# Sliding-window attention and a gated layer on one core: q and k loaded two tokens a partition, a narrower last stage, biases by ScalarE, the last block in halves

## The chip, the core and the metric

The kernel runs on one core of one Trainium2 chip. The metric is device microseconds of one execution, lower is better. The core has TensorE (PE; its weight loads are shown apart as PEld), VectorE (DVE), ScalarE (ACT), GpSimd (POOL) and SyncE (SP), each with an instruction queue worked off in order, and 16 DMA engines that move data between the device's memory (HBM) and the on-chip memory (SBUF). TensorE writes its results into PSUM, eight banks of 512 float32 columns on 128 partitions.

## What is computed

Attention over 8 batches, 8 heads, 576 tokens, head size 64, each token seeing itself and the 127 before it, with a bias that falls with the distance at a slope of its own for each head; then a gated layer over the 4608 tokens with all heads side by side (512 columns).

```python
scores = scale * np.matmul(q, k.transpose(0, 1, 3, 2))
bias = slopes[:, None, None] * (-np.abs(rel).astype(np.float32))[None, :, :]
mask = (rel >= 0) & (rel < window)            # window = 128
scores = np.where(mask, scores + bias[None], -1000000000.0)
...
attn = np.exp(scores)
attn = attn / (np.sum(attn, axis=-1, keepdims=True) + 1e-09)
x = np.matmul(attn, v)                        # then (B*S, H*D)
H = np.maximum(x @ w_h, 0.0)
T = 1.0 / (1.0 + np.exp(-(x @ w_t + b_t)))
out = T * H + (1.0 - T) * x
```

## The kernel before

**The order.** Nothing is scheduled by a planner at build time: `ORDER` (line 18) is a string of three-character steps, a letter and a two-digit number, and the loop at the end (line 433) issues them one after the other. Each engine works off its own steps in that order; semaphores hold a step until what it reads is there and what it overwrites has been read. `BANKS` (line 44) names the first PSUM bank of every tile in the order in which they are taken (`take`, line 247). The steps:

- `L`, `V`, `W`: loads of q or k, of v, of the weights (`load`, line 145), issued from POOL's queue, cast from float32 to bf16 on the way. `B` (line 224) loads the bias as float32 on all partitions from SP's queue.
- `T`: the transpose of a q or k tile on DVE (`tr`, line 233).
- `s`, `e`, `m`: scores on PE, exp on ACT, multiply by mask and bias table on DVE, one per stage (`scores`, `soft`, `mask`, lines 254 to 300). There are 32 stages, four per batch; each takes four PSUM banks, one for two heads: three stages of 2 x 192 columns a bank and a last one of 2 x 256.
- `p`, then `y` or `Y`: the two halves of P times V on PE for a block (`pv`, line 310; `Y` puts a drain of PE, a fence, ahead of the second half). There are 36 blocks of 128 tokens: four per batch, and one more per pair of batches made of both batches' last 64 tokens.
- `n`: division by the row sum on DVE. `x`, `c`: the block's transposes on PE and their copy by ACT. `h`: x times w_h on PE. `z`: x times w_t on PE, with the bias added by a fifth matmul against a matrix of ones (line 393), or, if `b` came before, onto the bias that ACT copied into the bank (`bias`, line 378; in 12 blocks).
- `u` or `U`: ReLU minus x, by DVE in one instruction (`u`, line 368), or ReLU by ACT (`U`, line 372) and the subtraction by DVE (`v`, line 374). `a`: tanh on ACT. `t` or `D`: half the tanh plus a half, by ACT or by DVE. `g` or `G`: the product, by DVE or POOL. `O` or `o`: plus x, by DVE or POOL. `d`: the store from SP's queue.
- `J`, `R`, `P`, `Q`, `S`, `r`, `I`, `k`, `K`: set-up, that is zeroing, the distances, the identity (`I`, on POOL), the tables (`k`, on ACT) and 22 matmuls on zeros that keep PE busy (`K`).

**q and k.** A load of one of them fills a tile of 4 heads by 32 partitions; a partition holds 18 neighbouring tokens (4608 bytes of HBM in one piece, 2304 bytes in SBUF). There are two tiles per batch and tensor, 32 loads and 32 transposes in all. The transpose takes 32x32 blocks of 4-byte pairs and writes token s*18+t of a block at place s*18+t, so neighbours of one block land 18 pairs, 72 bytes, apart. Tiles `LD` and `TR` (lines 110 and 112) are there twice, for even and odd batches: a load of batch b+2 waits for the transposes of batch b, a transpose for the scores of two batches earlier.

**v.** One load per batch into `va`, of 64-value rows; all eight batches have their own room. From the second part of the kernel on, a load of v starts behind a DVE operation named by `between` (line 137); POOL's gates and adds do so too.

**Start and end of the order:**

```
Q00L00B00R00S00L01r00L02L03J00k00P00K00L04L05L06L07T00V00T01W00L08T02I00W01T03s00W02T04s01e00L09T05e01s02V01T06 ...
... z35O33U35g34d33v35O34a35D35d34g35O35d35
```

Of the kernel before, what the change touches and what calls it, by code (L numbers as in the profile page):

```python
# [9 lines left out]
P = 128  # L10
# [4 lines left out]
ADD = ()  # L15
# [3 lines left out]
    "Q00L00B00R00S00L01r00L02L03J00k00P00K00L04L05L06L07T00V00T01W00L08T02I00W01T03s00W02T04s"  # L19
    "01e00L09T05e01s02V01T06e02s03T07e03L10m00s04m01s05e04m02L11m03p00e05p01Y00Y01n00p02L12n0"  # L20
    "1x00Y02c00p03n02x01V02h00c01m04x02y03c02h01n03U00s06m05L13x03L14e06z00T08h02c03T09a00s07"
    "t00v00z01u01e07g00m06h03U02p04m07a01p05Y04t01Y05n04z02U03G01b03n05z03L15a02T10V03x04p06a"
    "03T11p07c04Y06t02Y07n06z04o01n07s08a04D03x05v02e08x06D04x07T12h04c05s09v03c06m08h05c07T1"
    "3G03e09z05u04G02h06U05T14a05s10o00b06p08T15e10Y08o03d00z06d01n08U06L16s11m09a06x08e11m10"
    "h07v05z07u07o02c08s12a07m11L17d02p09d03e12p10Y09Y10G04n09t05s13n10L18p11e13o04T16Y11x09x"
    "10L19c09n11d04s14c10V04h08m12e14h09m13U08s15m14b08h10e15g05T17o05z08u10z09a08d05v06t06m1"
    "5p12a09p13Y12t07x11n12U09z10G07c11T18t09x12y13o07a10p14p15n13Y14b11Y15L20c12v08p16n14t10"
    "G06z11n15h11a11o06T19x13x14c13y16L21d06p17c14n16d07L22x15h12L23c15D11g10U11s16D08U12g08y"
    "17v09z12e16n17G09T20x16h13a12o08c16s17b14u13z13L24d08e17v11L25m16z14t12T21o10p18a13s18a1"
    "4m17L26Y18t13h14n18e18G13z15T22o09U14p19a15s19b16v12V05d09Y19m18e19d10z16n19h15o13T23a16"  # L30
    "x17x18c17p20L27g12U15T24Y20G11c18s20z17n20e20o11T25h16o12t15d11s21a17u16x19e21d12h17D14v"
    "14d13m19h18U17z18c19T26G14U18x20m20L28h19a18c20D16s22T27b19G16p21e22Y21u19o14z19n21s23L2"
    "9v15d14a19m21L30p22e23h20g15D17z20m22U20v17x21m23p23c21p24y22a20Y23n22o15z21n23o16d15p25"
    "a21y24Y25t18n24G17p26d16t19x22n25h21c22L31v18x23x24U21v20y26g19x25b22D20h22g18c23g20n26o"
    "17z22t21c24u22h23V06a22d17v21c25s24T28U23z23e24O19h24D22O18a23m24s25d18b24d19h25e25v23D2"
    "3z24G23u25U24T29x26z25G22c26a24T30s26o20a25z26e26T31d20h26m25a26s27U26g21m26p27e27p28Y27"
    "Y28v24n27o21t24n28s28V07d21x27e28v26p29g24x28m27Y29c27s29c28n29o22h27e29h28m28d22U27p30o"
    "23u28s30b27Y30e30o24d23x29n30z27c29v27d24s31m29a27z28e31m30h29D26D25g26a28g25p31m31p32t2"
    "8x30z29c30D27U29g28g27p33a29o25y31y32n31h30b30n32d25x31z30c31O28p34O26a30y33Y34U30D29d26"
    "n33p35t30h31v29g29x32z31v30c32n34o29b32x33u31y35c33x34o27n35z32a31g30h32d27a32D31d28g31c"  # L40
    "34d29z33O30t32O31d30U32x35h33a33d31v32c35g32z34D33U33O32v33h34d32a34g33h35t34u34z35O33U3"
    "5g34d33v35O34a35D35d34g35O35d35"
)
BANKS = (
    "1404040642740106057405613572357067450674075047506406540540567507256320742534074507640674"
    "0671450740574357045064520326105307546054067150750640754076407605730625723310567540271570"
    "1"
# [3 lines left out]
def lists():  # L51
# [8 lines left out]
    for b in range(NB):  # L60
        loads += [(w, b, g) for g in range(NG) for w in "kq"]
        loads += [("v", b)]
        if b == 0:
            loads += [("w", 0), ("w", 1), ("w", 2)]
# [8 lines left out]
def kernel(  # L73
# [55 lines left out]

    paired = [None]  # L130

    scaled = [None]

    def alone(ins):
        paired[0] = ins.ins
# [34 lines left out]
    def pads(i):  # L170
        for g in range(NG):
            for w in "qk":
                zero(TR[i, g, w][:, S:SQ, :])

# [303 lines left out]
```

## Time and profile before

| what | us |
|---|---|
| median of 3 runs | 156.6 |
| lowest and highest of them | 156.53 and 159.39 |
| the profiled execution | 156.13 |
| its span, first to last instruction | 154.2 |
| TensorE busy | 130.4 |
| VectorE busy | 136.0 |
| ScalarE busy | 121.3 |
| GpSimd busy | 80.8 |

The profile is of one execution. The 1.93 us between the execution and its span lie around the first and the last instruction. Busy times are unions of the engine's instructions; matmuls overlap each other, so the mean duration of one (380 ns for 512 columns) is longer than the pace at which they follow (four of them in 0.86 us). A group's line gives line number, engine, operation, output and input tiles and shapes, the count, then busy time and the mean of one in ns, then the idle time ahead of them and what ended it. The chain of work that ended last is followed back from the last instruction: at each step to what released it, or to the instruction before it on its engine; "issue" is time in which the engine waited for nothing that the profile shows. Tiles in PSUM are all called `ps`.

### The profile page before, as it was taken

The page shows a single profiled execution, that of the slowest core. Times are in us where ns is not written, and L with a number is a line of the kernel's source. Part 1 is how long each engine was busy: PE and PEld are TensorE (multiplying, and loading weights), DVE is VectorE, ACT ScalarE, POOL GpSimd, SP SyncE. Part 2 cuts the span into 40 slices and gives each one's busy share as a digit, 9 for nine tenths or more (in the row PEclk, how much of TensorE's full clock was granted, in tenths as well). Part 3 has the DMA queues.
Part 4 walks back from the last instruction along what each step waited for, and adds up shares of the span by engine and source line. Part 5 has one row for each costly group of instructions (what it writes and reads, how often), then busy time and mean ns, then how long its engine had stood idle before and what let it go on. Part 6 is the DMA issues. An engine that isn't in the chain of part 4 may idle for free.

```text
span 154.2 us, 6207 instructions
## 1 busy us (share of the span) xinstructions
PE 130.4 (85%) x2694; PEld 71.8 (47%) x2728; DVE 136.0 (88%) x257; ACT 121.3 (79%) x178; POOL 80.8 (52%) x90
## 2 busy tenths in 40 slices
PE   0598658698998999998999999989999799999930
PEld 0233326344554555465545545466445554555410
DVE  4999948398999899997999999989999979999880
ACT  3655972299579999994999999868999999868830
POOL 6984414402909479279488957554753771204000
PEclk9999995999999999999999999999999999999995
DMA  4999999999999759997999998786599199042732
GB/s 70 197 206 207 161 198 210 160 196 167 189 175 65 197 107 204 189 185 142 127 223 231 221 183 232 137 161 168 101 129 229 68 133 233 6 138 108 302 136 68
DMA packets 48106, 25.30 MB, mean 164 GB/s; under 512 B 38224, under 2 KB 39248, under 8 KB 48080
## 3 DMA queue, kind: packets, MB, share of 16 engines
q0 software_dynamic: 42688, 15.21, 91.6%
q1 hardware_dynamic: 5392, 9.70, 18.5%
q8 instruction: 21, 0.34, 0.9%
q14 instruction: 5, 0.04, 0.1%
HBM read 30.67 MB, written 9.44 MB: 260 GB/s over the span
## 4 chain that ended last, share of the span: by engine, by line
PE 70%; DMA 10%; issue 6%; DVE 6%; ACT 5%; DVEq 0%
PE ps L389 19%; PE ps L362 19%; PE ps L333 14%; DMA va<-in_v_dram 10%; PE ps L269 8%; PE ps L352 6%; PE ps L393 3%; ACT r L293 2%; ACT p L293 1%; DVE ot L417 1%; PE ps L279 1%; DVE p L168 1%; DVE uu L412 0%; DVE x L343 0%; ACT tt L402 0%
## 5 line engine op out<-in xcount | busy, mean ns | idle before, releaser
L417 POOL TENSOR_TENSOR ot<-uu,x 128x512 f32<-128x512 bf16 x26 | 29.8, 1155 | 23.8 <-DVE uu L376 9.6
L293 ACT ACTIVATE p<-ps 128x1536 bf16<-128x1536 f32 x24 | 34.7, 1457 | 4.6 <-PE ps L269 4.3
L362 PE MATMUL ps<-wH,xt 128*128 128x512 bf16 x130 | 35.3, 382 | 1.6 <-issue 1.0
L389 PE MATMUL ps<-wT,xt 128*128 128x512 bf16 x127 | 35.4, 380 | 1.1 <-issue 0.3
L412 POOL TENSOR_TENSOR uu<-uu,tt 128x512 bf16<-128x512 bf16 x14 | 16.1, 1153 | 23.8 <-ACT tt L402 10.6
L357 ACT COPY xt<-ps 128x512 bf16<-128x512 bf16 x36 | 20.6, 587 | 9.9 <-PE ps L352 9.7
L397 ACT ACTIVATE tt<-ps 128x512 f16<-128x512 f32 x36 | 21.6, 602 | 7.0 <-PE ps L393 4.7
L343 DVE TENSOR_TENSOR x<-ps,rd 128x512 bf16<-128x512 f32 x36 | 24.9, 691 | 2.1
L333 PE MATMUL ps<-va,p 64*128 64x65 bf16 x768 | 22.2, 193 | 3.9 <-DMA va<-in_v_dram 1.3
L300 DVE TENSOR_TENSOR p<-p,mk 128x1536 bf16<-128x1536 bf16 x24 | 22.8, 970 | 0.0
L333 PEld LDWEIGHTS <-p 64*128 64x128 bf16 x768 | 16.6, 95 | 12.6 <-issue 10.2
L362 PEld LDWEIGHTS <-xt 128*128 128x128 bf16 x144 | 13.0, 99 | 14.2 <-issue 1.8
L389 PEld LDWEIGHTS <-xt 128*128 128x128 bf16 x144 | 12.6, 98 | 12.9 <-issue 0.6
L154 POOL DMA_DIRECT2D va<-in_v_dram x8 | 14.8, 1851 | 1.9 <-DMA ld00k<-in_k_dram 1.0
L293 ACT ACTIVATE r<-ps 128x2048 bf16<-128x2048 f32 x8 | 15.0, 1874 | 0.5
L372 ACT ACTIVATE uu<-ps 128x512 bf16<-128x512 f32 x24 | 14.4, 604 | 1.0 <-PE ps L362 0.9
L352 PE MATMUL ps<-ident,x 128*128 128x128 bf16 x144 | 13.7, 225 | 1.5 <-issue 1.2
L342 DVE RECIPROCAL rd<-ps 128x8 f32<-128x8 f32 x36 | 7.1, 198 | 7.6 <-PE ps L333 7.1
L352 PEld LDWEIGHTS <-x 128*128 128x128 bf16 x144 | 9.5, 99 | 6.3 <-issue 1.9
L402 ACT ACTIVATE tt<-tt 128x512 f16<-128x512 f16 x19 | 11.9, 632 | 0.1
L242 PE MATMUL ps<-spin 128*128 128x512 bf16 x22 | 7.2, 503 | 5.4 <-DVE spin L168 5.4
L300 DVE TENSOR_TENSOR r<-r,mk 128x2048 bf16<-128x2048 bf16 x8 | 10.3, 1294 | 0.3 <-ACT r L293 0.3
(77 smaller groups left out, 195.2 us busy)
## 6 DMA issues: line engine op xcount, KB each, us to landing
out_dram<-ot SPq DMA_DIRECT2D x32, 256.0 KB, 4.0
va<-in_v_dram POOLq DMA_DIRECT2D x8, 576.0 KB, 10.9
ld00k<-in_k_dram POOLq DMA_DIRECT2D x4, 288.0 KB, 5.7
ld00q<-in_q_dram POOLq DMA_DIRECT2D x4, 288.0 KB, 6.0
ld01k<-in_k_dram POOLq DMA_DIRECT2D x4, 288.0 KB, 6.1
ld01q<-in_q_dram POOLq DMA_DIRECT2D x4, 288.0 KB, 7.1
ld10k<-in_k_dram POOLq DMA_DIRECT2D x4, 288.0 KB, 5.8
ld10q<-in_q_dram POOLq DMA_DIRECT2D x4, 288.0 KB, 7.5
```

The costliest lines, as they stand in the source:

```text
L154: ins = nc.gpsimd.dma_start(out=va[:, b, :, 0:D], in_=v[b].rearrange("h s d -> (h s) d").rearrange("(n p) d -> p n d", p=P))
L293: nc.scalar.activation(out=pview(b, s), in_=SC.pop((b, s))[:, :, 0:n].rearrange("p h (g n) -> p h g n", g=NG), func=ACTF.Exp, scale=scale)
L300: alone(nc.vector.tensor_tensor(out=p, in0=p, in1=(MK3 if s == 3 else MK)[:], op=ALU.mult))
L333: mm = nc.tensor.matmul(out=av[o : o + m, par, j * (D + 1) : (j + 1) * (D + 1)], lhsT=PT[bb, st][rows, h, c : c + m], rhs=VA[bb][rows, at ...
L343: nc.vector.tensor_tensor(out=x[:].rearrange("p (i r d) -> p r i d", i=NH, r=2), in0=av[:, :, :, 0:D], in1=rd[:].to_broadcast([P, 2, NH, D ...
L352: nc.tensor.transpose(out=pt[:, c * P : (c + 1) * P], in_=X[b, s][:, c * P : (c + 1) * P], identity=ident[:])
L357: nc.scalar.copy(out=xt[:].rearrange("p c n -> p (c n)"), in_=XP.pop((b, s)))
L362: nc.tensor.matmul(out=pa, lhsT=XT[b, s][:, c, :], rhs=wH[:, c, :], start=c == 0, stop=c == NC - 1)
L389: nc.tensor.matmul(out=pz, lhsT=xt[:, c, :], rhs=wT[:, c, :], start=c == 0 and not given, stop=c == NC - 1 and given, skip_group_check=given)
L397: nc.scalar.activation(out=tt[:], in_=PZ.pop((b, s)), func=ACTF.Tanh, scale=0.5)
L412: note(eng.tensor_tensor(out=uu, in0=uu, in1=TT.pop((b, s))[:], op=ALU.mult))
L417: note(eng.tensor_tensor(out=ot[:], in0=UU.pop((b, s))[:], in1=X[b, s][:], op=ALU.add))
```

## The change

Five edits and a new `ORDER` and `BANKS` (both strings are left out below).

- q and k: batch 0 is loaded as before, into halves of a wider tile. For batches 1 to 7 a load brings 2 heads into 32 partitions, a partition getting 18 pieces of 2 tokens (512 bytes of HBM each, 256 in SBUF); four loads fill a tile of all 8 heads, and one transpose per tensor turns it. `L` goes from 32 to 60, `T` from 32 to 18. A transpose of batches 1 to 7 has 1152 pairs a partition, and neighbours land 2 pairs, 8 bytes, apart. Heads lie in another order in the tiles, which `scores`, the tables and `pv` follow.
- The last stage of a batch: 448 columns instead of 512 (the last 64 tokens against themselves once, each of the two head groups on its own half of the partitions). Exp writes a tile of its own (`E3`), and the multiply is two instructions into `PE3`; the second table `MK3` (8 activations to set up) gives way to a small `MT`.
- `b` goes from 12 to 32 blocks; `z` of the other 4 keeps the matmul.
- The last block of all (35): after the first half of its columns come steps `f`, `w`, `q`, `j`, `l`, which do h, u, g, O and the store for columns 256 to 511. One of its two row halves is stored from ACT's queue.
- The bias load `B` waits for the latest transpose of batch 0 (`turned`); the tiles `xt` have six buffers instead of four; an option that was switched off (`ADD`, `additive`) is gone.

The new order moves work between engines. Steps of each kind:

| step | L | T | b | u | U | v | D | t | g | G | O | o | Y | y |
|---|---|---|---|---|---|---|---|---|---|---|---|---|---|---|
| before | 32 | 32 | 12 | 12 | 24 | 24 | 17 | 19 | 22 | 14 | 10 | 26 | 25 | 11 |
| after | 60 | 18 | 32 | 28 | 8 | 8 | 20 | 16 | 27 | 9 | 12 | 24 | 31 | 5 |

Its start and its end:

```
L00P00L01L02J00S00R00K00L03L04r00L05k00L08T00L09Q00L06L07L10T02T01L11T03V00s00B00s01W00e00W01e01s02W02V01T04s03e02T05L12e03L13m00s04m01s05e04m02L16m03I00p00 ...
... z35t34u34g34d33h35a35o34f00u35t35w00g35d34q00O35j00d35l00
```

```diff
     for b in range(NB):
-        loads += [(w, b, g) for g in range(NG) for w in "kq"]
+        loads += [(w, b, h) for w in "kq" for h in (0, 2, 1, 3)] if b else [
+            (w, b, g) for g in range(NG) for w in "kq"]
...
-    fx = ctx.enter_context(tc.tile_pool(name="fx", bufs=4))
+    fx = ctx.enter_context(tc.tile_pool(name="fx", bufs=6))
...
     def load(kind, *at):
         if kind in "qk":
-            b, g = at
+            b, h = at
+            if b == 0:
+                half = LD[0, kind][:].rearrange("p n x -> p (n x)")[:, h * NT * D : (h + 1) * NT * D]
+                nc.gpsimd.dma_start(
+                    out=half, in_=(q if kind == "q" else k)[0, h::NG].rearrange(
+                        "h (s t) d -> h s (t d)", t=NT))
+                return
             nc.gpsimd.dma_start(
-                out=LD[b % 2, g, kind][:],
-                in_=(q if kind == "q" else k)[b, 4 * g : 4 * g + 4].rearrange(
-                    "h (s t) d -> (h s) (t d)", t=NT))
+                out=LD[b % 2, kind][32 * h : 32 * h + 32],
+                in_=(q if kind == "q" else k)[b, NG * h : NG * h + NG].rearrange(
+                    "g (n s t) d -> s (g n) (t d)", s=32, t=2))
...
     def tr(w, b, g):
...
         nc.vector.transpose(
-            out=TR[b % 2, g, w][:, 0:S].rearrange("p s e -> p (s e)").bitcast(U32).rearrange(
-                "p (s t) -> p t s", t=NT),
-            in_=LD[b % 2, g, w][:].bitcast(U32).rearrange("p (t i) -> p t i", i=32))
+            out=TR[b % 2, w][:, 0 : NG * S].rearrange("p s e -> p (s e)").bitcast(U32).rearrange(
+                "p (n s t) -> p n t s", s=32, t=2),
+            in_=LD[b % 2, w][:].rearrange("p n x -> p (n x)").bitcast(U32).rearrange(
+                "p (n t i) -> p n t i", t=2, i=32))
...
     def mask(b, s):
-        p = pview(b, s)
-        alone(nc.vector.tensor_tensor(out=p, in0=p, in1=(MK3 if s == 3 else MK)[:], op=ALU.mult))
+        p = pview(PT[b, s])
+        if s < 3:
+            alone(nc.vector.tensor_tensor(out=p, in0=p, in1=MK[:], op=ALU.mult))
+            return
+        e3 = E3[b % 2]
+        nc.vector.tensor_tensor(out=p, in0=e3[:, :, 0:384].rearrange("p h (g n) -> p h g n", g=NG),
+                                in1=MK[:], op=ALU.mult)
+        alone(nc.vector.tensor_tensor(out=PT[b, s][:, :, 576:640], in0=e3[:, :, 384:448], in1=MT[:], op=ALU.mult))
...
+    LAST = (NB // 2 - 1, NS)
+
+    def cols(b, s, half):
+        if (b, s) != LAST:
+            return slice(0, DM)
+        return slice(half * DM // 2, (half + 1) * DM // 2)
...
+            eng = nc.scalar if r and (b, s) == LAST else nc.sync
+            eng.dma_start(out=out[row : row + D, at], in_=ot[r * D : (r + 1) * D, at])
+
+    second = dict(f=mm_h, w=lambda b, s, half: relu_sub(b, s, "u", half), l=store,
+                  q=lambda b, s, half: gate(b, s, "g", half), j=lambda b, s, half: add_x(b, s, "O", half))
```

## The prediction

> **What bounds the kernel now.** I read the page's busy times first, then the chain of work that ended last, then busy times by stretch of the span, then the groups with shapes kept apart.
>
> ```profile
> PE 130.4 (85%) x2694; PEld 71.8 (47%) x2728; DVE 136.0 (88%) x257; ACT 121.3 (79%) x178; POOL 80.8 (52%) x90
> ...
> q0 software_dynamic: 42688, 15.21, 91.6%
> ...
> PE 70%; DMA 10%; issue 6%; DVE 6%; ACT 5%; DVEq 0%
> ```
>
> By busy time VectorE leads; by the chain TensorE does. The chain from 0 to 36 us and its lines from 32 to 146 us say which holds where:
>
> ```profile
> 6.80 15.12 DMA va<-in_v_dram
> 21.93 0.14 issue
> 22.06 0.55 PE ps L333 x24
> ```
> ```profile
> by line: PE ps L389 25.8%; PE ps L362 23.7%; PE ps L333 16.6%; PE ps L269 10.4%; PE ps L352 7.0%; issue 4.7%; PE ps L393 4.3%; ACT r L293 3.2%; ACT p L293 1.3%; PE ps L279 1.3%; ACT tt L402 0.6%; ACT xt L357 0.5%; ACT tt L397 0.4%; ACT uu L
> ```
> ```profile
> 32.00:142.00 110.00, 103.75 (x2262) 58.33 (x2289) 104.55 (x184) 98.30 (x141) 63.91 (x62) 1.00 1.09 159
> ```
>
> Three stages. Until 22.06 us TensorE's P times V waits for the first v load: issued at 6.80 us, behind eight q, k loads, landed 15.12 us later. From there to about 146 us TensorE's own matmuls are 89% of the chain (25.8+23.7+16.6+10.4+7.0+4.3+1.3). The last row (length, then busy PE, PEld, DVE, ACT, POOL) shows VectorE as full as TensorE, 104.55 and 103.75 of 110 us, and ScalarE at 98.30. So PE sets the end, and DVE would as soon as it got more work. The tail runs from the last matmul near 147.8 us to 154.2. The profiled execution took 156.13 us (span 154.2 and 1.93 around it), 0.3% under the median 156.6; I sum against 156.13.
>
> **The change part by part.** Prices:
>
> ```profile
> L368 DVE SCALAR_TENSOR_TENSOR uu<-ps,x 128x512 bf16<-128x512 f32 x12 | 8.2, 683 | 0.6 <-PE ps L362 0.4
> L376 DVE TENSOR_TENSOR uu<-uu,x 128x512 bf16<-128x512 bf16 x24 | 10.3, 431 | 0.2 <-ACT uu L372 0.2
> L393 PE MATMUL ps<-bT,ones 128*128 128x512 bf16 x24 | 9.1, 379 | 0.2 <-issue 0.2
> L380 ACT COPY ps<-bA 128x512 f32<-128x512 f32 x12 | 7.2, 601 | 0.2
> L372 ACT ACTIVATE uu<-ps 128x512 bf16<-128x512 f32 x24 | 14.4, 604 | 1.0 <-PE ps L362 0.9
> L234 DVE STREAM_TRANSPOSE tr10k<-ld10k 128x576 uint32<-128x576 uint32 x4 | 5.0, 1253 | 0.0
> L168 DVE MEMSET bT<- 128x256 uint32 x1 | 0.3, 272 | 0.0
> L181 DVE MEMSET va<- 128x288 bf16 x1 | 0.3, 298 | 1.0 <-issue 1.0
> L148 POOL DMA_DIRECT2D ld10k<-in_k_dram x4 | 2.3, 571 | 1.3 <-DVE rd L342 1.3
> L160 POOL DMA_DIRECT2D wH<-in_moe_w_h_dram x1 | 0.8, 779 | 0.0
> L154 POOL DMA_DIRECT2D va<-in_v_dram x8 | 14.8, 1851 | 1.9 <-DMA ld00k<-in_k_dram 1.0
> ```
>
> Transposes. 28 of 1.245 us (34.9 us) become 14 of 1152 elements. The old row costs 2.06 ns an element after some 0.05 us; the memset of 256 uint32 costs 1.06 with everything in it. What sets the transpose apart from the engine's other rows is where it writes: neighbouring elements 72 bytes apart (18 tokens of 4 bytes). The new one writes them 8 bytes apart. Lower end: 1.06 ns, 1.22 us each. Upper end: 2.06 ns, 2.42 us. Both a contiguous write and a 4-byte element at 1.06 ns exist (L168), so I take 1.25 us: 14 x 1.25 = 17.5, DVE -17.4 us. Against it stands L181, which writes 130 bytes apart and still takes 298 ns for 288 elements: a wide step alone need not cost double. At the upper end DVE gains 1.0 us only. The Trainium skill ("SBUF — State Buffer", Specifications) says that a 16-byte line needs two hits for full bandwidth; by that, 72 bytes pay and 8 bytes do not, and the sum would be the lower end's. L181 is a row that disagrees with it, the 2.06 ns one that agrees.
>
> ReLU moved. U (ScalarE, then v on DVE) falls 24 to 8, u (DVE alone) rises 12 to 28: ACT -16 x 0.604 = -9.7, DVE 16 x (0.683 - 0.431) = +4.0.
>
> Bias by ScalarE, 12 to 32: ACT +20 x 0.601 = +12.0. PE loses 20 of 24 bias matmuls; on the chain these are 4.3% of 114 us = 4.9 us, so 20/24 of it, -4.1 us, lies on the path.
>
> Gates and adds. D 17 to 20, t 19 to 16: ACT -1.9, DVE +0.85. G 14 to 9: POOL -5.8, DVE +5 x 0.416 = +2.1. o 26 to 24: POOL -2.3, DVE +2 x 0.682 = +1.4. Halves of the last block: DVE +0.4.
>
> Last stage of a batch. Exp over 1792 columns: between the rows for 1536 (1.457 us) and 2048 (1.874), 1.67: ACT 8 x -0.2 = -1.7. The multiply is one of 1536 (0.970) and one of 256 (0.28, from 0.970 at 1536 and 0.416 at 512) against 1.294: nothing. The 16 extra score matmuls stay 16. The table set-up loses 8 activations (ACT -2.1) in front of the first exp, which waited for PE anyway: no gain.
>
> Sums. DVE after the start: -17.4+4.0+0.85+2.1+1.4+0.4 = -8.7 us; at the transpose's upper end +7.7. ACT in the steady stage: +12.0-9.7-1.9-1.7 = -1.3. PE: -4.1.
>
> POOL. 28 issues of 128 rows (0.57) become 56 of 576 pieces. Between 0.57 and v's 1.85 (4608 pieces); nearest is the weight's 0.78 (512 pieces), so 0.8: 44.8 - 16.0 = +28.8, with the gates and adds +20.7, 101.5 us in all. It is an in-order queue on which G, o and the loads wait for each other; room is there (63.91 of 110 us busy). What hangs on it is the stores, and the six `ft` buffers: if its adds come later than that, tanh and ReLU wait for a buffer.
>
> DMA. Bytes stay; packets on q0 go to 42688 - 28 x 128 + 56 x 576 = 71,360. The trace's packet records: 128-byte packets take 31 ns and start at up to 1,208 per us, 2304-byte ones 192 ns and 92 per us, that is 13.2 and 174 ns of an engine each. A line between puts 256 bytes at 23 ns by rate, 41 ns by duration. q and k of a batch: 4608 packets over 16 engines, 6.6 us (by duration 11.8) against 5.6 now. The steady stage has the room (the transfers' bytes pass well under the 233 GB/s of the best slice); the start has not: batch 1 lies ahead of the first v. +1.0 us there, up to +6; the bias broadcast (256 KB, now issued behind the first transposes) leaves the start, -0.7. Net +0.3, and +0.2 for the smaller pieces' issue: V00 +0.5 us. The queue's SP side: the bias load now waits some 12 us on SP, with no store behind it before about 41 us.
>
> Order. The identity's select on POOL now stands behind V01 and three loads; it is needed by the first block transpose near 24 us, and POOL's issues up to it sum to about 18 us from 1.3 us on (12 loads 8.7, v 3.7, weights 2.1, three loads 2.4, the iota 0.6), so it stays hidden, with some 4 us to spare; beyond that it delays PE one for one. Fenced P times V: 25 to 31; a fence shows as 0.08 us of "issue" (22.61 us in the chain): +0.5.
>
> Gaps. In the steady stage 12.4 of 114 us on the chain are not matmuls (issue 5.4, ACT 7). Bounds: nothing to half. With DVE 8% lighter, six `fx` buffers for four, and ACT no fuller, I take a fifth: -2.5.
>
> Tail. Last DVE work after the last matmul: now tanh 0.60, scale 0.29, gate 0.42, add 0.69; then two stores issued by SP in 1.12 us. After: ReLU half 0.42, two gate halves 0.28, two add halves 0.41, the last stores half as large and on two queues. Between -1.4 and 0: -0.8.
>
> Sum: 156.13 - 4.1 - 2.5 - 0.8 + 0.5 + 0.5 = 149.7 us.
>
> **The rivals.**
> (1) Slower: the transposes keep 2.06 ns an element. DVE is busy 113.63 us between 22 and 146 us by the stretches; with 7.7 more it needs 128 us at the 95% it reaches now, 132 at its mean 92%, against 124: 160 to 164 us, say 162. For it: no row shows this operation faster; L181. Against: no other DVE row of 500 elements or more takes over 1.4 ns an element. It decides from about 1.9 us a transpose on, where DVE has as much work as before.
> (2) Loads late. POOL's waits show each issue held until the load eight before it landed:
>
> ```profile
> POOL ld01q L148 <- DMA va<-in_v_dram: 5.1, 1, 5.1
> POOL wT L160 <- DMA ld01q<-in_q_dram: 0.3, 1, 0.3
> ```
>
> Eight loads are now half the bytes, V02 stands behind all of batches 2 and 3, and v takes 8.6 to 18.8 us to land. If packets add up by duration (11.8 us a batch), V00 is 5 us late, or V02 stalls PE as much: 154 us. Against: 128-byte packets overlap 2.4 deep in the records. The Trainium skill ("SBUF — State Buffer", Door 1: The DMA port swizzle) says that 32 partitions reach 8 of 16 ports, 189 GB/s against 328; no transfer of before has 32 partitions, so no row here can show it. It would make this case.
> (3) The gain does not come: a bias by ScalarE holds its PSUM bank from the copy on, so 20 more blocks hold one longer and ACT's in-order queue waits; the 4.1 us return as waits: 155 us. The 12 present copies wait 0.2 us in all, which speaks against.
>
> **How the numbers follow.** Forecast 149.7: 0.68, own range 145 (half of the gaps gone, tail at its best) to 153.4. Rival 1: 0.16, rival 2: 0.10, rival 3: 0.06. The range 145 to 158 takes in 2 and 3 and leaves out most of 1. Faster by over 2% (under 153.5; 2% is about what a measurement of this kernel can tell from no change): 0.68; within 2%: 0.16; slower: 0.16.
>
> **What would show it.** A transpose row 128x1152 near 1.25 us; DVE near 127, POOL near 101 us; four bias matmuls left; the v piece of the chain ending near 22.5 us; matmuls still about 89% of the chain behind it. Wrong if transposes take over 1.9 us, if DMA pieces appear in the chain after 30 us, or if ScalarE's bias copies wait.

## The result, and the profile after

The changed kernel takes 165.0 us (median of 4 runs, 164.17 to 167.42) against 156.8 us for the kernel before on the same chip: 1.051 times the time, 95% interval 1.046 to 1.057. It is slower; the forecast was 149.7 us, range 145 to 158. Some executions run longer than the others of their kernel, a few of them far longer: they count in medians and ranges, but not in the ratios. The profiled execution took 165.12 us, span 163.4. Of its page, the lines that answer to those shown in the prediction:

```profile
PE 131.1 (80%) x2712; PEld 72.5 (44%) x2712; DVE 130.7 (80%) x265; ACT 118.8 (73%) x171; POOL 95.5 (58%) x111
...
q0 software_dynamic: 73344, 15.22, 121.4%
...
PE 58%; DMA 16%; DVE 7%; issue 7%; ACT 6%; POOL 2%; DVEq 0%; POOLq 0%
```

VectorE did get lighter (136.0 to 130.7 us), and GpSimd's queue fuller (80.8 to 95.5). But no engine is full any more: TensorE falls from 85% to 80% of the span, and on the chain from 70% to 58%, while DMA grows from 10% to 16%. The chain (start, length, what) has the loss at two places. The start:

```profile
1.35 9.63 DMA ld0k<-in_k_dram
...
16.52 10.59 DMA va<-in_v_dram
...
27.25 0.30 PE ps L344 x8
```

The first P times V comes at 27.25 us, where before it came at 22.06. And the middle:

```profile
55.01 1.16 POOL uu L434
56.17 0.66 POOL ld0k L156
56.83 1.31 POOL ld0q L156 x2
58.15 0.57 POOL ld0k L156
58.79 5.90 DMA ld0k<-in_k_dram
```

At 55 us the chain runs over a gate on GpSimd; four loads are issued behind it, and for the last of them the issue of a transpose waits. This piece of the chain runs beside busy engines: from 54.1 to 64.8 us no idle time of TensorE is over 0.3 us. Busy times by stretch (length, then PE, PEld, DVE, ACT, POOL, clock, DMA share, GB/s), after first, then before:

```profile
32.00:92.00 60.00, 48.91 (x1078) 27.08 (x1077) 47.46 (x82) 45.63 (x65) 40.75 (x48) 1.00 1.88 162
92.00:142.00 50.00, 47.96 (x1104) 27.59 (x1103) 48.18 (x95) 45.94 (x64) 29.04 (x29) 1.00 1.26 155
```
```profile
32.00:92.00 60.00, 56.19 (x1251) 31.41 (x1266) 56.82 (x92) 54.30 (x77) 38.79 (x39) 1.00 1.32 175
92.00:142.00 50.00, 47.56 (x1013) 26.92 (x1024) 47.73 (x93) 43.99 (x65) 25.11 (x23) 1.00 0.82 140
```

From 92 us on the two kernels are alike. Between 32 and 92 us TensorE is busy 48.91 of 60 us where it was busy 56.19, at the same clock, and VectorE loses as much: both wait. Only DMA is busier (share 1.88 for 1.32), and it moves fewer bytes a second (162 for 175 GB/s). What TensorE's idle time in this stretch ends on (us in total, times, longest) is, in the changed kernel:

```profile
PE ps L344 <- issue: 2.9, 4, 1.0
PE ps L275 <- issue: 2.6, 2, 1.7
PE ps L363 <- DVE p L306: 2.3, 1, 2.3
PE ps L363 <- issue: 1.7, 1, 1.7
```

That is 7.2 us in which TensorE waits for nothing that the profile shows (1.4 in the kernel before), most of it inside groups of equal matmuls, and 2.3 us for a multiply of VectorE. None of it ends on a load. VectorE's idle time in the stretch ends on TensorE (6.9 and 4.5 us), and no part of it on a load either. So a late load, the first guess for the middle, is not what the engines wait for there in this execution; the question comes back at the end.

To see where a kernel falls behind, TensorE's weight loads of each trace were counted, each weighted with the time that its matmul takes of TensorE, and the times compared at which the same share of that work had begun (all columns but the first are differences from it; the last three are experiments told of below):

| share of PE's work | before, us | after | p2_wide | h1_fourheads | h3_split |
|---|---|---|---|---|---|
| 3% | 22.2 | +5.5 | +0.6 | +1.1 | -0.4 |
| 15% | 40.8 | +5.4 | +2.6 | +1.8 | -1.1 |
| 25% | 53.5 | +7.2 | +4.5 | +4.5 | -0.5 |
| 45% | 79.0 | +11.9 | +5.9 | +7.2 | +0.9 |
| 60% | 98.4 | +10.9 | +9.4 | +6.7 | +1.2 |
| 99% | 145.9 | +10.6 | +11.9 | +9.5 | +1.2 |

So the change loses 5.5 us before 28 us and 6.5 more between 46 and 91 us; it wins back 1.3 from there on, and 1.4 behind the 99% (6.9 us to the end of the span where before took 8.3), which leaves the 9.2 us between the spans.

### The profile page after: what moved, and what is told of

It reads as the page before. It is cut to its first block, busy times and chain, and to the rows that moved or that the text cites. A ratio compares the mean times of both kernels' runs of the same rounds, so it can differ in the third digit from the quotient of the medians.

```text
span 163.4 us, 6278 instructions
## 1 busy us (share of the span) xinstructions
PE 131.1 (80%) x2712; PEld 72.5 (44%) x2712; DVE 130.7 (80%) x265; ACT 118.8 (73%) x171; POOL 95.5 (58%) x111
## 4 chain that ended last, share of the span: by engine, by line
PE 58%; DMA 16%; DVE 7%; issue 7%; ACT 6%; POOL 2%; DVEq 0%; POOLq 0%
PE ps L410 17%; PE ps L381 16%; PE ps L344 13%; DMA ld0k<-in_k_dram 10%; DMA va<-in_v_dram 6%; PE ps L275 6%; PE ps L363 5%; ACT p L301 3%; DVE p L306 2%; DVE tr0k L236 1%; ACT e L301 1%; ACT xt L368 1%; POOL ld0q L156 1%; DVE tr1k L243 1%; DVE r L176 1%
## 5 line engine op out<-in xcount | busy, mean ns | idle before, releaser
L441 POOL TENSOR_TENSOR ot<-uu,x 128x512 f32<-128x512 bf16 x24 | 27.5, 1152 | 34.6 <-DVE uu L434 13.2
L410 PE MATMUL ps<-wT,xt 128*128 128x512 bf16 x144 | 36.5, 380 | 0.0
L381 PE MATMUL ps<-wH,xt 128*128 128x512 bf16 (+1 forms) x148 | 36.4, 374 | 0.0
L344 PE MATMUL ps<-va,p 64*128 64x65 bf16 x768 | 23.8, 196 | 5.4 <-DMA va<-in_v_dram 1.8
L390 DVE SCALAR_TENSOR_TENSOR uu<-ps,x 128x512 bf16<-128x512 f32 (+1 forms) x29 | 19.2, 668 | 6.3 <-PE ps L381 5.9
L434 POOL TENSOR_TENSOR uu<-uu,tt 128x512 bf16<-128x512 bf16 x9 | 10.4, 1157 | 16.2 <-DVE tt L425 13.1
L401 ACT COPY ps<-bA 128x512 f32<-128x512 f32 x32 | 19.1, 603 | 0.3
L275 PE MATMUL ps<-tr0q,tr0k 32*64 32x192 bf16 x512 | 10.1, 266 | 7.5 <-DVE tr0q L236 6.6
L301 ACT ACTIVATE e<-ps 128x1792 bf16<-128x1792 f32 x8 | 13.3, 1665 | 1.1 <-PE ps L285 0.9
L156 POOL DMA_DIRECT2D ld1k<-in_k_dram x16 | 10.7, 673 | 5.2 <-DMA ld0k<-in_k_dram 3.7
## 6 DMA issues: line engine op xcount, KB each, us to landing
va<-in_v_dram POOLq DMA_DIRECT2D x8, 576.0 KB, 11.1
```

Source lines behind the costliest of these rows:

```text
L275: nc.tensor.matmul(out=sc[half * D : (half + 1) * D, h, g * pitch : g * pitch + 192], lhsT=TR[b % 2, "k"][rows, g0 + t * D : g0 + (t + 1) ...
L301: nc.scalar.activation(out=out, in_=in_, func=ACTF.Exp, scale=scale)
L344: mm = nc.tensor.matmul(out=av[o : o + m, par, j * (D + 1) : (j + 1) * (D + 1)], lhsT=PT[bb, st][rows, h, c : c + m], rhs=VA[bb][rows, at ...
L381: nc.tensor.matmul(out=pa, lhsT=XT[b, s][:, c, :], rhs=wH[:, c, at], start=c == 0, stop=c == NC - 1)
L390: nc.vector.scalar_tensor_tensor(out=uu, in0=pa, scalar=0.0, in1=X[b, s][:, at], op0=ALU.max, op1=ALU.subtract)
L410: nc.tensor.matmul(out=pz, lhsT=xt[:, c, :], rhs=wT[:, c, :], start=c == 0 and not given, stop=c == NC - 1 and given, skip_group_check=given)
```

## The experiments

The theory that the runs were made for: loads come late, at the start because of the shape of batch 0's loads, in the middle because pieces of two tokens fill the DMA queue and GpSimd's in-order queue. Rivals: the packets are innocent and the new order costs by itself; the bias copies by ScalarE hold it up; the mere number of loads does. Each run was timed beside the kernel before on its chip; a ratio is to that kernel, with its 95% interval.

### The start: e2_every2 and e1_alike

e2_every2 is the kernel before with batch 0's heads exchanged (every second head to a load, as the change has it).

```diff
+            if b == 0:
+                nc.gpsimd.dma_start(
+                    out=LD[0, g, kind][:], in_=(q if kind == "q" else k)[0, g::NG].rearrange(
+                        "h (s t) d -> h s (t d)", t=NT))
+                return
```

> The kernel before with one edit: batch 0's q and k are taken from every second head (4 x 32 rows that cannot be merged) instead of four neighbouring heads (128 rows). Batch 0's heads are exchanged in the result; the bytes, the tiles and the order are the same. Theory (few engines): the first load lands some 5 us later, the first v near 27 us, the time is about 161. Rival (set-up): no change, 156.6.

Measured: 159.7 us, ratio 1.024 (1.017 to 1.031), some 3.7 us at the same bytes and packets, with the changed kernel's first wait on its chain:

```profile
1.33 10.74 DMA ld00k<-in_k_dram
```

The page's list of loads (KB each, median us from issue to landing) has for batch 0 of the changed kernel, and for four batches of the kernel before (of these, batch 0's own four loads landed 4.9 to 6.7 us after their issue):

```profile
ld0k<-in_k_dram POOLq DMA_DIRECT2D x2, 288.0 KB, 10.3
ld0q<-in_q_dram POOLq DMA_DIRECT2D x2, 288.0 KB, 11.0
```
```profile
ld00k<-in_k_dram POOLq DMA_DIRECT2D x4, 288.0 KB, 5.7
ld00q<-in_q_dram POOLq DMA_DIRECT2D x4, 288.0 KB, 6.0
```

In the trace's packet records 2304-byte packets start at 92 per us before, and in the changed kernel's start at 21 per us at first, about a quarter (up to 76 once several loads are under way). A source of heads 0, 2, 4, 6 is four pieces of 32 rows that do not join, and so is a load with four parts outermost. The Trainium skill ("DMA: Bandwidth & Descriptors", Rules for kernel authors, the row on using all 16 engines) says that an outermost dimension of size c under 16 confines a load to at most c engines. With c = 4 the 21 per us agree. So the batch-0 loads that I costed as unchanged ("loaded as before") explain over half of the 5.5 us.

e1_alike is the changed kernel with batch 0 in two-token pieces too (eight loads on 32 partitions, two wide transposes).

```diff
-        loads += [(w, b, h) for w in "kq" for h in (0, 2, 1, 3)] if b else [
-            (w, b, g) for g in range(NG) for w in "kq"]
+        loads += [(w, b, h) for w in "kq" for h in ((0, 2, 1, 3) if b else ((0, 2), (1, 3)))]
```

> The changed kernel with batch 0 loaded like the others: two tokens a partition, 32 partitions a load (eight loads, two wide transposes), nothing else moved. Theory (few engines): batch 0's loads have 4 x 32 rows on the HBM side, and each is moved by a few DMA engines only, so the first landed at 11.0 us and the first v at 27.1; with 32 rows outermost they spread, the first v lands near 22.5 us and the time falls from 165 to about 160.5. Rival (set-up): the start is late because of the zeroing that VectorE does first and of POOL's longer issues; then the first v stays near 27 us and the time near 165.

Measured: 161.5 us, 3.1% over the kernel before by the medians (four executions from 157.4 to 162.1 us, no interval). At 3% of the work it is 3.3 us late instead of 5.5. The start is cured in part.

### The loads and the rest, each without the other

p2_wide: the kernel before in its own order, with only q and k changed from batch 1 on (two-token pieces, two loads in the place of each, wide transposes); batch 0 as before.

```diff
+            if b:
+                part, kind = (kind == "q"), "kq"[g]
+                for h in (2 * part, 2 * part + 1):
+                    nc.gpsimd.dma_start(
+                        out=LDW[b % 2, kind][32 * h : 32 * h + 32],
+                        in_=(q if kind == "q" else k)[b, NG * h : NG * h + NG].rearrange(
+                            "g (n s t) d -> s (g n) (t d)", s=32, t=2))
+                return
```

> The kernel before, in its own order, with the other part alone: q and k of batches 1 to 7 come in two-token pieces, two loads at each place of one, k's first, and 14 wide transposes of 1.37 us take the place of 28 of 1.24 (15.6 us less on VectorE, 28 more loads on POOL, 256-byte packets); batch 0 as before; the first load of batch 2 goes two steps later, and from batch 1 on the heads go with other slopes and other v, with the same work. If the small pieces and the doubled loads are what makes the changed kernel late between 46 and 91 us, this loses 4 to 8 us (160 to 164); if the new order is, it stays within 2 us of the kernel before or gains. Since four heads a load with the new order gave 163.6, I take the order: 156.

Measured: 166.7 us, ratio 1.051 (1.037 to 1.064), that is 8.0 us of 156.9 (5.9 to 10.1). My choice (156) was wrong. The loads cost by themselves, in an order that has nothing new. (The run with four heads a load, on which I had leaned, is h1_fourheads, told of below.) The q0 line of p2_wide and the longest pieces of its chain from 28 to 110 us:

```profile
q0 software_dynamic: 71808, 15.21, 136.1%
```
```profile
23.27 14.07 DMA va<-in_v_dram
...
42.36 12.23 DMA ld1q<-in_q_dram
...
60.87 5.67 DMA ld0k<-in_k_dram
...
90.94 1.83 POOL ot L437
92.77 1.56 POOL va L166
...
96.40 8.00 DMA ld0q<-in_q_dram
```

Transfers of v, k and q, 6 to 14 us each, are on the path far behind the start, and around 90 us GpSimd itself. Here the engines do wait for them. VectorE's idle time ahead of three groups of transposes (us in total, times, longest) went on the load:

```profile
DVE tr1q L248 <- DMA ld1q<-in_q_dram: 2.7, 1, 2.7
DVE tr1k L248 <- DMA ld1k<-in_k_dram: 1.5, 1, 1.5
DVE tr0q L248 <- DMA ld0q<-in_q_dram: 1.1, 2, 0.7
```

TensorE waits 1.8 us for v there. In the kernel before neither of the two waits for a load between 28 and 110 us. (p2_wide's chain is 34% DMA, that of before 10%; this execution took 167.9 us, somewhat above the median, and its clock was 0.93 from 92 to 142 us, so its column in the table ends too high.)

h3_split: the kernel before with every load of q and k from batch 1 on split in two of 64 partitions; packets, transposes and order stay.

```diff
-            nc.gpsimd.dma_start(
-                out=LD[b % 2, g, kind][:],
+            for m in range(1 if b == 0 else 2):
+                n = 4 if b == 0 else 2
+                nc.gpsimd.dma_start(
+                    out=LD[b % 2, g, kind][32 * n * m : 32 * n * (m + 1)],
...
```

> The kernel before, with each load of q and k from batch 1 on split in two of 64 partitions, issued one behind the other: 28 more loads on POOL, 0.6 us each, or 17 us of POOL's time, and half-size loads among the eight outstanding; order, packets and transposes as before. If the number of half-size loads delays the work by POOL's queue, this is 3 to 6 us slower than before (160 to 162); if it is not the number, at most 1 us slower.

Measured: 157.1 us, ratio 1.003 (0.998 to 1.007). The number of loads, with 14 us more on GpSimd, costs nothing that can be measured. That rival falls for the old order; what costs in p2_wide is what the loads are made of, or that a wide transpose needs four of them.

h1_fourheads: the other half, the changed kernel with loads and transposes undone for all batches (four neighbouring heads, 128 partitions, 2304-byte packets).

```diff
-                out=LD[b % 2, kind][32 * h : 32 * h + 32],
-                in_=(q if kind == "q" else k)[b, NG * h : NG * h + NG].rearrange(
-                    "g (n s t) d -> s (g n) (t d)", s=32, t=2))
+                out=LD[b % 2, kind][:].rearrange("p n x -> p (n x)")[:, h * NT * D : (h + 1) * NT * D],
+                in_=(q if kind == "q" else k)[b, 4 * h : 4 * h + 4].rearrange(
+                    "h (s t) d -> (h s) (t d)", t=NT))
```

> The changed kernel with its loads and transposes undone for all eight batches: a load again brings four heads that lie side by side (128 partitions, 2304-byte packets, four loads a batch), and each is transposed by itself at about 1.24 us; the order, the banks, the 32 biases by ScalarE, the 448-column stage and the halves stay. The heads go with other slopes and other v than in the reference, with the same amount of work. If the loads are what costs (small pieces, half-size loads, 32 partitions), this falls below the kernel before, 150 to 156 us: the start as before, and the 2.5 us that the biases gain in the second half. If the new order and the rest lose the time between 46 and 91 us, as the runs with 18 tokens a piece hint, it stays above 160 us. I take 157, with the loads as the larger share.

Measured: 163.6 us (the median of four, one of them 297.5), ratio 1.039 (1.032 to 1.046); I had taken 157. The start is right again (+1.1), and the middle is still lost. VectorE (third number) between 44 and 92 us, in the changed kernel and here:

```profile
44.00:92.00 48.00, 39.76 (x854) 21.78 (x855) 39.52 (x68) 38.24 (x56) 34.34 (x40) 1.00 1.85 170
```
```profile
44.00:92.00 48.00, 41.10 (x913) 22.21 (x912) 46.66 (x81) 39.38 (x56) 24.13 (x27) 1.00 1.26 171
```

DMA is as idle as it was in the kernel before (1.26; there 1.22), and VectorE is busy 46.66 of 48 us where the changed kernel's is busy 39.52. With the narrow transposes VectorE has 141.3 us of work in all, for 136.0 in the kernel before: the new order gives it more than it has room for. So, as far as this trace shows, the order needs the cheap transposes, and these come only with the small pieces.

### Larger pieces

e3_three: three tokens a piece instead of two (384-byte packets). g2_eighteen: e1_alike with 18 tokens a piece (2304-byte packets on 32 partitions) in all batches; g1_mixed: in batches 0 to 3 only; h2_twoheads: 18 tokens, and 64 partitions a load. One number changes:

```diff
-                    "g (n s t) d -> s (g n) (t d)", s=32, t=2))
+                    "g (n s t) d -> s (g n) (t d)", s=32, t=3))
...
-                "p (n t i) -> p n t i", t=2, i=32))
+                "p (n t i) -> p n t i", t=3, i=32))
```

> The changed kernel with three tokens a piece instead of two: pieces of 768 bytes (384 in SBUF), 384 per load for 576, neighbours 12 bytes apart in the transpose. Theory (crowded DMA): fewer packets (about 21,500 for 32,256) let PE's gaps inside a group of matmuls fall from 7.5 to about 5 us and the loads land earlier: about 162 if the transpose stays near 1.4 us. If the transpose pays for every line that it crosses, it takes 1.7 to 2.4 us, VectorE gets 5 to 14 us more work, and the time is 163 to 168. Rival (order): packets do not matter, the time follows the transpose alone, 165 or more.

> The kernel of e1_alike (161.5) with 18 tokens a piece for batches 0 to 3 and two from batch 4 on: still 32 partitions and two heads a load, but 64 packets of 2304 bytes for 576 of 256. Six to eight of the sixteen transposes write 72 bytes apart again and take about 2.45 us for 1.37 (+8.6 us on VectorE in the first half). Theory (DMA is the bound of the first 70 us): large pieces move a batch's q and k in 5.6 us for 7, the loads are on time, and the time falls to 154 to 157 in spite of VectorE's work. Rival (the order or POOL's queue makes the loads late): it stays at 160 or more, VectorE adding to it.

> The same with 18 tokens a piece in all batches: the change without its small pieces, with the old price of the transpose (16 wide ones of about 2.45 us, VectorE +17 us on e1_alike, some 148 us in all). Theory: VectorE becomes the bound of the second half, 160 to 164. If TensorE alone sets the pace of the second half, 155 to 157.

> As the run with four heads a load, but from batch 1 on a load brings two heads to 64 partitions: eight loads a batch of the size and at the places of the changed kernel, in 2304-byte packets. Against the run with 18 tokens a piece in all batches (166.4 us) it differs in the partitions of a load, 64 for 32, and in two narrow transposes for one wide one (2.5 for 2.3 us). If loads of 32 partitions are what costs, it stands within 2 us of the run with four heads; if the number of half-size loads in POOL's queue, with only eight outstanding, is what costs, it stays near 166; if neither, all three are alike. I take the number of loads, 162.

Measured: 163.4 us, ratio 1.046 (1.038 to 1.053); 166.1 us, 1.066 (1.056 to 1.077); 166.4 us, 1.063 (1.051 to 1.075); 165.2 us, 1.051 (1.045 to 1.057). Large packets bring nothing. e3_three came as expected; g1_mixed, g2_eighteen and h2_twoheads were slower than I had put them. A transposed tile of 1152 pairs costs, with three tokens and with 18:

```profile
L244 DVE STREAM_TRANSPOSE tr1k<-ld1k 128x1152 uint32<-128x1152 uint32 x4 | 7.0, 1753 | 2.5 <-DMA ld1k<-in_k_dram 2.5
```
```profile
L238 DVE STREAM_TRANSPOSE tr1k<-ld1k 128x1152 uint32<-128x1152 uint32 x4 | 9.3, 2335 | 0.9 <-DMA ld1k<-in_k_dram 0.9
```

and g2_eighteen's VectorE is where that of h1_fourheads was, with DMA relieved:

```profile
44.00:92.00 48.00, 39.03 (x823) 21.20 (x833) 44.93 (x66) 37.16 (x53) 29.44 (x37) 0.96 1.30 167
```

With small pieces VectorE stands idle 8.5 of the 48 us (in the changed kernel's trace for TensorE, 5.3 and 2.3 us, not for a load), with large ones it is nearly full, and TensorE gets about as far in either case (39.76, 39.03, 41.10 of 48 us). These runs refute "larger packets cure it"; they do not clear the packets, since none has large packets and cheap transposes together: the tokens of a piece set both.

### What else is in the queue: e4_nov, e7_b_nov, f1_v02, f2_gates

e4_nov is the changed kernel without the loads of v of batches 2 to 7 (it multiplies by the v of batches 0 and 1), e7_b_nov the kernel before without them.

```diff
             b, = at
+            if b > 1:
+                return
...
-    VA = [va[:, i] for i in range(NB)]
+    VA = [va[:, i % 2] for i in range(NB)]
```

> The changed kernel without the loads of v for batches 2 to 7 (their P times V takes the v of batches 0 and 1): 27,648 packets of 128 bytes fewer, all other work as it was. Theory (crowded DMA): what is lost behind the start is lost to loads and instruction fetches that queue behind small packets; the time falls to 156 to 159. Rival (order): the new order and the biases on ScalarE make the engines wait for each other; the time stays at 163 to 165.

> The kernel before without the loads of v for batches 2 to 7 (batches 0 and 1's v in their place), as in e4_nov: the control for it. Theory (DMA is the bound of the changed kernel's first 70 us, not of the kernel before behind its start): 155.5 to 156.7, at most 1 us less, where the changed kernel lost 4.8. Rival (v's loads hold up either kernel alike): 152 or less.

Measured: 160.2 us, ratio 1.016 (1.005 to 1.027), by the ratios some 5.5 us less than the changed kernel (4.8 by the medians); and 155.2 us, 0.993 (0.989 to 0.997), 1.2 us less than the kernel before. The same loads left out are worth over four times as much after the change: its loads are a limit behind the start, those of before hardly. With them go the packets and some 11 us of GpSimd's issuing in either kernel, and the two runs do not tell these apart. In the changed kernel the late v shows on GpSimd (start, length, what, in brackets the wait ahead):

```profile
37.58 1.15 POOL L434 TENSOR_TENSOR uu<-uu,tt 128x512 bf16<-128x512 bf16 x1 [7.65 <-DVE tt L425]
38.68 0.72 POOL L156 DMA_DIRECT2D ld0k<-in_k_dram  x1
...
47.05 1.83 POOL L162 DMA_DIRECT2D va<-in_v_dram  x1
```

A gate waits 7.65 us for VectorE, eleven loads of q and k and a second gate stand behind it, and V02 goes out at 47.05 us (25.77 in the kernel before). TensorE waits 2.3 us for this load in e1_alike's trace and 2.1 in f3_pebias's (told of below), but not in the changed kernel's own.

f1_v02 is e1_alike with V02 issued ahead of that gate and of batch 3's loads; f2_gates is e1_alike with all nine gates of GpSimd on VectorE (`G` to `g` in the order).

> The kernel of e1_alike (161.5 us median) with one step moved: the load of batch 2's v is issued ahead of block 0's gate on POOL and of all of batch 3's loads, where it stood behind ten loads and two gates. Theory (late loads): in e1_alike PE waited 2.3 us for this load at 53.5 us, and the engines lost 3.7 us on the kernel before between 48 and 65 us; that wait goes, the time falls by 2 to 4 us, to 157.5 to 159.5. Rival (order): the wait moves to another step, 161 as before.

> The kernel of e1_alike with all nine gates of POOL done by VectorE at the same places of the order (VectorE 9 x 0.42 = +3.8 us, POOL -10.4 us). Theory (late loads): block 0's gate held POOL's queue for 7.9 us and block 2's for 3.3 us with loads behind them; without it all loads are issued up to 8 us earlier, the wait for v goes, and the time falls by 2 to 4 us although VectorE has more to do. Rival (VectorE): 3.8 us more on VectorE cost as much, the time stays or rises to 163.

Measured: 164.9 us, ratio 1.059 (1.053 to 1.065), 3.4 us more than e1_alike: my expectation failed. With v moved up, a transpose waits 3.2 us for batch 2's q, and TensorE as long for the transposed tile at 45 us: here the wait only moved. f2_gates: 158.4 us, 1.016 (1.011 to 1.021), the best of the changed kernels that do all the work. With the start of e1_alike and no gate ahead of its loads, most of the loss is gone, though the packets of batches 1 to 7 are those of the changed kernel: between 32 and 92 us its TensorE is back at 54.11 of 60 us, with DMA as busy as ever (1.94). So the same packets need not cost what they cost the changed kernel. It is still slower than the kernel before. What the gates alone are worth is not shown: against e1_alike it is 3.1 us by the medians, but one of e1_alike's four executions, at 157.4 us, was faster than all of f2_gates (157.9 to 158.8).

f4_both does f1 and f2 at once, g3_mixed_gates does g1 and f2.

> The kernel of e1_alike with both edits, v of batch 2 moved up and the nine gates on VectorE. Theory (late loads): the loads are no longer late anywhere; what stays is the start, about 3 us later than before, and TensorE's own saving of 4: 155 to 157. Rival: VectorE's 3.8 us more, 159 to 161.

> g1 with the nine gates of POOL done by VectorE (+3.8 us on VectorE). If POOL's queue still delays loads in g1, it gains up to 2 us on g1; if DMA is no longer the bound there, VectorE's work shows, and it loses 1 to 3 us on g1.

Measured: 165.0 us, ratio 1.044 (1.032 to 1.056), and 168.5 us, 1.067 (1.048 to 1.085). Both scatter by 6 us and more and settle nothing beyond that neither is a cure; what I expected of f4_both failed.

### The biases: f3_pebias, p1_biases, p3_both

f3_pebias is the changed kernel with 20 biases given back to TensorE (the bank is taken where it was).

```diff
         pz = PZ[b, s] = take(1)[:, 0, :]
+        if by["b"].index((b, s)) not in KEPT:
+            BY_PE.add((b, s))
+            return
         nc.scalar.copy(out=pz, in_=bA[:])
```

> The changed kernel (165.0) with the biases of the 20 blocks put back on TensorE: their steps b only reserve the PSUM bank, the bias is added by the fifth matmul as before. TensorE +4.3 us, ScalarE -12 us. Theory of the prediction (TensorE sets the pace): the time rises by the 4.1 us that I took off for them, to 169. Rival (the gain was lost because ScalarE's in-order queue takes 12 us more): the time falls, 161 to 164. In between, 165 to 167, TensorE is not the bound where the loads are late, and the biases were worth only part of it.

Measured: 165.4 us, ratio 1.065 (1.056 to 1.075), against 1.051 (1.046 to 1.057): 1.4% or some 2 us worse by the ratios, at most 2.9%, and 0.4 us by the medians. So TensorE's 20 matmuls are worth less than the 4.1 us that I took off, but how much less is open. Nor does the run say that TensorE's work no longer counts: its trace has 5.2 us more of busy TensorE (136.3 for 131.1), and also lacks the changed kernel's waits for nothing shown (between 32 and 92 us TensorE is idle 4.9 us for 11.1). The two may cancel.

p1_biases is the kernel before with the 20 biases by ScalarE, p3_both adds them to p2_wide; each `b` step is put in behind the last earlier step that takes a bank. Some of the biases do not come through in these two; the instructions are as many.

> The kernel before, in its own order, with one part of the change alone: the 20 biases that TensorE adds there are brought by ScalarE (32 in all), each copy put behind the last earlier step that takes a bank, so that the banks stay as they are. TensorE loses 20 matmuls of 0.206 us, 4.1 us; ScalarE gains 20 copies of 0.60 us, 12.0 us over 133 us at 78%. If the part is worth what the prediction gave it, 152 to 153.5 us; if the copies, in an order that was not made for them, hold ScalarE or a bank, 156 to 160. I take 154.5.

> Both parts at once in the order of the kernel before: two-token pieces with wide transposes, and 32 biases by ScalarE. It is the change without its new order, its 448-column stage and its halves. If the order is what costs, 152 to 156 us, faster than the kernel before or equal; if the loads are, 158 to 163. I take 154.

Measured: 163.9 us, ratio 1.040 (1.030 to 1.049), and 167.5 us, 1.053 (1.040 to 1.067). In the old order the copies cost 6.2 us (4.0% of 156.9) instead of gaining 4.1. Whether it is the copies or the places I chose for them is not parted: the one profiled execution of p1_biases took 243.6 us and is no guide. On top of p2_wide they change nothing that can be measured. Of both runs I had expected 154 to 155.

## Why the prediction was wrong

**The step that failed** is the paragraph on DMA: "The steady stage has the room (the transfers' bytes pass well under the 233 GB/s of the best slice); the start has not", with its sum "V00 +0.5 us", and with it the term that was to profit from the room, "Gaps -2.5". In their place the runs showed V00 +5.2, and in the steady stage 7.3 us more of idle TensorE between 32 and 92 us (11.1 for 3.8) where 2.5 were to go.

**V00 +0.5.** Measured +5.2 (27.25 against 22.06 us). The batch-0 loads, which I did not look at since they were "as before", are the larger part (e2_every2: 3.7 us by themselves). With the half-size loads behind them, the first v went out at 16.52 us instead of 6.80. This part is shown.

**Room in the steady stage.** Room was judged by bytes, and by GpSimd's busy time; for small packets neither is the measure. (The page's row of GB/s has slices up to 302, too; 233 is not the best.) My own rates (13.2 ns of an engine for 128 bytes, 174 for 2304) held, and the traces have 22.9 (p2_wide) to 24.4 ns for 256 bytes where I put 23. By them q and k of a batch cost 6.6 to 7.0 us of DMA instead of 5.6. I charged that once, at the start; it is paid for seven batches, 7 to 10 us in all. The trace's packets, summed by these rates, take 70 to 99% of the 16 engines from 10 to 55 us in the changed kernel, and 94 to 100% from 10 to 45 us before: the full stretch is 10 us longer. p2_wide, which has nothing else of the change, lost 8.0 us (5.9 to 10.1), and its VectorE and TensorE do wait for loads. That the two are of one size may be chance, since some of the packets' time is hidden and a wide transpose also waits for four loads; that the loads cost that much alone, in the old order, the run shows. In the new order it depends on what stands around them: f2_gates has the same packets from batch 1 on and loses 1.6% in all.

**Gaps -2.5.** How the middle's 6.5 us come about in the changed kernel stays open. Leaving out six loads of v gives some 5.5 us back, so the loads have a part in it; but in its trace TensorE's idle time from 32 to 92 us ends on nothing shown (7.2 us) and on a multiply (2.3 us), and never on a load. That the middle is lost to late loads is argued from p2_wide, e4_nov and f2_gates, not read from the changed kernel.

**The transposes** were right: 1.37 us against 1.25 forecast, far from the 2.42 of rival 1.

```profile
L243 DVE STREAM_TRANSPOSE tr1k<-ld1k 128x1152 uint32<-128x1152 uint32 x4 | 5.5, 1373 | 2.9 <-DMA ld1k<-in_k_dram 2.9
...
L401 ACT COPY ps<-bA 128x512 f32<-128x512 f32 x32 | 19.1, 603 | 0.3
...
L156 POOL DMA_DIRECT2D ld1k<-in_k_dram x16 | 10.7, 673 | 5.2 <-DMA ld0k<-in_k_dram 3.7 <-DMA ld0q<-in_q_dram 1.6
```

VectorE ends at 130.7 us for 127 forecast, GpSimd at 95.5 for 101 (a load's issue is 0.67 us, not 0.8). But a lighter VectorE was to shorten the gaps of TensorE's chain (-2.5). It only waits longer, busy 47.46 of 60 us from 32 to 92 us. The 2.9 us ahead of the transposes at the end of the first line are a wait for a load, but one that ended at 20.2 us, in the start.

**The biases -4.1.** The matmuls went (x24 to x4), and ScalarE's copies wait 0.3 us, so rival 3's sign did not come. But the term is a share of a chain on which TensorE has to be the bound, and from 32 to 92 us it is idle 11.1 of 60 us. f3_pebias puts the worth of the biases at 1.4% of the time, between nothing and 2.9% (4.1 us would be 2.6%).

**The fences +0.5, the tail -0.8.** Behind 92 us the two kernels run alike, with 1.3 us won up to 99% of the work for all these terms together. The end is the one term that came better than forecast: -1.4 behind the 99%.

**The rivals.** Of the rivals only number 2, at chance 0.10, had its sign come: DMA pieces in the chain after 30 us. V00 came 5 us late, too, as it says, but mostly from batch 0's loads and not from packets that add up by duration: that the size agrees is luck. It was priced at 154 us, one late v, and left out the steady stage. The rule of the Trainium skill which I named there ("SBUF — State Buffer", Door 1: The DMA port swizzle: 32 partitions reach half of the ports) is not borne out as the cause. At 18 tokens a piece, loads of 32, 64 and 128 partitions give 166.4, 165.2 and 163.6 us (ratios 1.063, 1.051, 1.039): the order does not speak against the rule, but the steps are small, VectorE is nearly full in all three, and they differ in their transposes too. In the records the 2304-byte packets start as fast with 32 partitions a load (g2_eighteen, up to 93 per us) and with 64 (h3_split, 94) as with 128 (the kernel before, 95), and h3_split's time is the kernel before's. No run has 256-byte packets on more than 32 partitions a load.

**What stays open.** How p2_wide's 8 us divide between the packets' time, the 32 partitions, and the wait of one transpose for four loads. And the gaps inside groups of equal matmuls, such as this one of the changed kernel:

```profile
32.25 0.21 PE ps L275 x5
32.46 1.67 issue
34.13 0.54 PE ps L275 x24
```

They add up to 7.5 us in its trace, 1.65 in that of before, 2.5 in e1_alike and 0.5 in f3_pebias (which does 5.2 us more of matmuls). So they are most of what TensorE lost between 32 and 92 us, and the strongest rival to late loads there. All but the first (0.5 us at 16.8 us, in f3_pebias as well) begin 0.9 to 2.5 us behind the start of a 16 KB transfer of the queue q8, "instruction", which takes no longer than before (median 1.07 us for 1.06). They do not go with small pieces as such: p2_wide has none over 0.3 us, g2_eighteen with large packets has 6.4 us. That TensorE waits for its program there is only argued. It was not tried.

## What to carry to other kernels

Before loads are cut into smaller pieces, sum the packets' engine time for every batch, not the bytes, and not for the start alone, and look at what stands ahead of the loads in their queue. A load "as before" whose source changes its outermost dimension is a new load: cost it. The engine time that a change saves is worth little where the engine stands idle anyway; ask what must hold for a saving to reach the path, and take it off the sum if the change itself upsets that. And a piece of DMA on the chain is not yet a wait: look at whether the engines were idle beside it, and what that idle time ended on.

## What the runs showed of the hardware

- The price of a transpose of 128x1152 4-byte pairs goes by the step at which it writes: 1.37 us at 8 bytes, 1.75 at 12, 2.31 to 2.34 at 72 bytes. The Trainium skill ("SBUF — State Buffer", Specifications) has 16-byte lines that want two hits for full bandwidth; the order of the three agrees, the 12-byte step lying between.
- Batch 0's loads from four separate pieces of 32 rows landed 9.6 to 11.0 us after their issue, those of 128 joined rows with the same bytes and packets 4.9 to 6.7.
- Issuing a load costs GpSimd 0.57 us with 128 pieces of 2304 bytes, 0.67 with 576 of 256 bytes, 1.85 with 4608 of 128 bytes.
- Splitting 28 loads in two of 64 partitions changed the time by 0.3% (-0.2 to +0.7), though in the waits that the profile shows GpSimd holds an issue until the eighth load before it has landed.
